# Other slots for the attention visits in the first looped row of an attention-and-MLP kernel

## The chip, the cores and the metric

The kernel runs on one core of a Trainium2 chip. The metric is the device time of one execution in microseconds (us).

## What is computed

The reference has two parts. A linear attention with a decaying state runs over 4 batches, 8 heads, 768 positions and 48 channels, all in float32:

```python
for t in range(S):
    cur = u * k[t] (outer) v[t]
    y[t] = r[t] @ (state + cur)
    state = w[t][:, None] * state + k[t] (outer) v[t]
```

Its output, as 3072 rows of 384, goes through a gated MLP: `(sigmoid(x @ w_gate) * (x @ w_val)) @ w_out`, with 1536 hidden columns.

## The kernel before

**Chunks and rows.** The attention is cut into 24 chunks of 128 positions of one batch. Chunk q belongs to batch q % 4 and to row q // 4, so a row of the MLP is four chunks, 512 tokens. Row n of the MLP can only run when the four chunks of row n are done. A prologue, whose order a planner makes from costs and due times (`Plan`, lines 154 to 199, `add` calls of lines 606 to 681), does chunks 0 to 7, prepares chunk 8, brings in chunk 9's data and computes row 0 of the MLP. The change doesn't touch it.

**The loop.** Rows 1 to 5 run in a written-out loop (lines 761 to 786). A row has 12 steps, one for each 128 hidden columns, and a step has four slots. At each slot, work of the attention that was noted for it is issued first; then comes the step's own work: after slot 0 the gate product (`gate`, PE into `pg`, lines 525 and 528) and its sigmoid (ACT, L538); after slot 1 the value product (PE into `pu`), then `hidden` (DVE, L545), `hidden_hi` (ACT, L549) and `hidden_lo` (DVE, L553); after slot 2 the down product of the step before (PE into `po`, L568); after slot 3 nothing. Slots are counted from the start of the first looped row (row 1), 48 to a row. All engines work their queues in the order of issue.

**The attention's work on chunk q+1 and on chunk q.** `prepare(q + 1, early, turn, late, more)` (line 718) issues, at slot `early`, two products on POOL (`bonus1`, `bonus2`, L319 and L322, which read `tok`), `prep_k` on DVE (a scan L339, a reciprocal L343, a product L345, which read and write `pin`) and `fade` (DVE, L351); at slot `turn` the PE transposes `turn_k` (L370 into `pk`) and their copy `take_k` on ACT (L374 into `kT`); at slots `late` and `more` `prep_r` (DVE, L356 and L361), `guard` (ACT, L365), `bonus3` (DVE, L326) and `bonus4` (POOL, L332). A **visit** of chunk q (line 746) is `both(q)`: 160 small PE products (L418, L431 for chunk q; L389, L402 for chunk q+1), then `take_y` (ACT, L476), `mask`, `middle` and `keep` of chunk q+1 (DVE, L458, L469, L473) and, on SP's queue, the loads of `pin` (L301) and `tok` (L306) for chunk q+2. Three slots later come `turn_x` (PE, L481), `take_x` (ACT, L504) and `rest_x` (DVE, L514). `pin` and `tok` have two buffers each, so the load of chunk q+2 waits until the visit of chunk q has read them. `kT` and `eg` have one buffer, and so has the PSUM bank that `pk`, `py` and `px` take in turn.

**The first looped row.** Chunk 8 has no visit before it, so its transposes stand at slot 1 and its scores and sums (`section1`, L389 and L402) at slot 3 (lines 739 to 742). Four weight blocks are still to be split there: `w_hi` (ACT, L284) and `w_lo` (DVE, L287) at slots 1 and 2, 5 and 6, 9 and 10, 13 and 14 (lines 756 to 758). In rows 2 to 5 the visits stand at slots 7, 19, 31 and 43 of the row, and each chunk is prepared at 7, 5, 3 and 3 slots before the visit that needs it. Row 1 has a table of its own:

```python
visit = {q: (q - start) // B * row + (7 + 12 * (q % B) if q >= start + B else FIRST[q - start]) for q in range(start, NG)}
...
prepare(q + 1, *EARLY[q - start] if q < start + B else (time - 7, time - 5, time - 3, time - 3))
```

Of the kernel before, what the change touches and what calls it, by code (L numbers as in the profile page):

```python
# [41 lines left out]
LATE = dict(b3=-1.05, wl=-28.0, xl=26.5)  # L42
ROOM = dict(pin=2, tok=2, bon=2, eg=1, ready=2, mid=1, kT=1, at=2, pair=1, bank=1, x=2, temp=1, pg=1, pu=1, unit=2)
R0 = 1
FIRST = [11, 21, 32, 43]
EARLY = [(4, 6, 8, 8), (12, 16, 17, 17), (23, 27, 28, 28), (34, 38, 39, 39)]
HC = C // 2
HALVES = [slice(0, HC), slice(HC, C)]
HW = 3 * DM // 2
# [155 lines left out]
def tile_kernel(ctx: ExitStack, tc: tile.TileContext, dec: bass.AP, tok: bass.AP, wts: bass.AP, u: bass.AP, out: bass.AP):  # L205
# [509 lines left out]
    def at(time, f, *a):  # L715
        todo.setdefault(time, []).append((f, a))

    def prepare(q, early, turn, late, more):
        at(early, bonus1, q)
        at(early, bonus2, q)  # L720
        at(early, prep_k, q)
        at(early, fade, q)
        at(turn, turn_k, q)
        at(turn, take_k, q)
        at(late, prep_r, q)
        at(late, guard, q)
        at(more, bonus3, q)
        at(more, bonus4, q)
# [8 lines left out]
    start = (R0 + 1) * B  # L737
    visit = {q: (q - start) // B * row + (7 + 12 * (q % B) if q >= start + B else FIRST[q - start]) for q in range(start, NG)}
    at(1, turn_k, start)
# [3 lines left out]
    for q, time in visit.items():  # L743
        if q + 1 < NG:
            prepare(q + 1, *EARLY[q - start] if q < start + B else (time - 7, time - 5, time - 3, time - 3))
        at(time, both, q)
# [78 lines left out]
```

## Time and profile before

| | us |
|---|---|
| median of 3 runs | 583.19 (582.59 to 584.51) |
| profiled execution, its own time | 585.22 |
| span of its instructions | 582.9 |
| PE busy | 547.9 (94%) |
| DVE busy | 324.0 (56%) |
| ACT busy | 204.7 (35%) |
| POOL busy | 100.7 (17%) |
| mean granted TensorE clock | 0.991 |

PE is TensorE's matmul, PEld its weight load, DVE VectorE, ACT ScalarE, POOL GpSimd, SP SyncE, whose queue issues the loads. L568 is line 568 of the kernel. A tile's name stands without its buffer number. An arrow is read "written from"; "<-" behind an idle time names what ended it. All times within the trace are counted from the first instruction.

### The profile page before, as it was taken

How to read it: one execution, taken by the hardware profiler on the slowest of the kernel's cores; microseconds unless marked ns; L12 is line 12 of the kernel's file. 1: busy time of each engine (PE TensorE's matmuls, PEld its weight loads, DVE VectorE, ACT ScalarE, POOL GpSimd, SP SyncE). 2: the span in 40 equal slices, each digit the busy share in tenths (PEclk: the TensorE clock that was granted, in tenths of full speed). 3: DMA queues.
4: the chain of work that ended last, by engine and by line, in shares of the span. 5: the costliest groups of instructions: out<-in, count | busy, mean ns of one | idle time of the engine just before them, and what ended most of it. 6: DMA issues, size and time to landing. Idle time of an engine off the chain costs nothing.

```text
span 582.9 us, 13165 instructions
## 1 busy us (share of the span) xinstructions
PE 547.9 (94%) x5864; PEld 449.3 (77%) x5864; DVE 324.0 (56%) x451; ACT 204.7 (35%) x376; POOL 100.7 (17%) x89
## 2 busy tenths in 40 slices
PE   3698899999889999999999999999999999999995
PEld 2577687887767888877888888888888888888884
DVE  4998999996754654644535545645545521222221
ACT  2557765744432323422223333223323322321221
POOL 4350533104010210210121221211220200000000
PEclk9999999999898999999999999999999999999998
DMA  8748827324020232231130330230330200100001
GB/s 253 256 170 284 251 93 305 76 77 147 12 90 15 76 89 60 84 90 40 51 90 12 110 113 13 77 90 15 112 107 19 72 3 1 55 1 1 0 1 60
DMA packets 11044, 50.57 MB, mean 87 GB/s; under 512 B 1265, under 2 KB 1266, under 8 KB 9442
## 3 DMA queue, kind: packets, MB, share of 16 engines
q1 hardware_dynamic: 8818, 45.70, 25.0%
q10 hardware_dynamic: 2160, 3.93, 1.7%
q8 instruction: 48, 0.79, 0.6%
q14 instruction: 18, 0.15, 0.1%
HBM read 44.91 MB, written 4.72 MB: 85 GB/s over the span
## 4 chain that ended last, share of the span: by engine, by line
PE 86%; DVE 6%; DMA 3%; issue 2%; ACT 1%; POOL 1%; SPq 0%; DVEq 0%; ACTq 0%
PE po L568 24%; PE pg L525 16%; PE pu L525 15%; PE pg L528 8%; PE pu L528 8%; PE py L431 3%; PE py L418 3%; DMA pin<-dec 3%; PE pg L522 2%; PE pk L370 2%; PE pa L389 2%; PE pa L402 1%; PE px L481 1%; DVE raw L275 1%; PE po L564 1%
## 5 line engine op out<-in xcount | busy, mean ns | idle before, releaser
L545 DVE TENSOR_TENSOR sg<-pu,sg 128x512 f32<-128x512 f32 (+1 forms) x76 | 50.3, 661 | 166.8 <-PE pu L528 162.1
L568 PE MATMUL po<-hh,w 128*128 128x512 f32 x408 | 130.3, 401 | 0.0
L525 PE MATMUL pg<-x,w 128*128 128x512 f32 x408 | 107.5, 399 | 0.0
L525 PE MATMUL pu<-x,w 128*128 128x512 f32 x408 | 105.0, 393 | 0.0
L525 PEld LDWEIGHTS pu<-x,w 128*128 128x128 f32 x408 | 76.8, 189 | 16.2
L525 PEld LDWEIGHTS pg<-x,w 128*128 128x128 f32 x408 | 74.9, 188 | 16.2
L568 PEld LDWEIGHTS po<-hh,w 128*128 128x128 f32 x408 | 75.1, 190 | 14.2
L549 ACT CAST hh<-sg 128x512 fp32r<-128x512 f32 x68 | 42.2, 620 | 123.0 <-DVE sg L545 122.9
L538 ACT ACTIVATE sg<-pg 128x512 f32<-128x512 f32 (+1 forms) x76 | 43.5, 572 | 115.2 <-PE pg L528 110.8
L568 PE MATMUL po<-hl,w 128*128 128x512 f32 x204 | 80.2, 393 | 0.1
L553 DVE TENSOR_TENSOR hl<-sg,hh 128x512 fp32r<-128x512 f32 x68 | 50.2, 738 | 42.2 <-ACT hh L549 42.2
L319 POOL TENSOR_TENSOR bon<-tok,ub 128x384 f32<-128x384 f32 x24 | 30.7, 1280 | 237.1 <-DMA tok<-tok 170.7
L528 PE MATMUL pg<-x,w 128*128 128x512 f32 x204 | 58.3, 394 | 0.0
L528 PE MATMUL pu<-x,w 128*128 128x512 f32 x204 | 57.6, 390 | 0.0
L332 POOL TENSOR_TENSOR at<-eye,a 128x512 f32<-128x512 f32 x24 | 31.5, 1314 | 126.2 <-DVE a L326 126.2
L568 PEld LDWEIGHTS po<-hl,w 128*128 128x128 f32 x204 | 38.6, 189 | 9.2 <-DVE hl L553 0.6
L528 PEld LDWEIGHTS pg<-x,w 128*128 128x128 f32 x204 | 38.7, 190 | 8.4
L528 PEld LDWEIGHTS pu<-x,w 128*128 128x128 f32 x204 | 38.3, 188 | 8.0
L339 DVE TENSOR_TENSOR_SCAN eg<-pin,ends 112x516 f32<-112x516 f32 x24 | 34.7, 1446 | 9.5 <-DMA pin<-dec 9.5
L365 ACT ACTIVATE eg<-eg 112x1032 f32<-112x1032 f32 x24 | 25.6, 1067 | 31.1 <-DVE pin L361 29.8
L322 POOL TENSOR_TENSOR bon<-bon,tok 128x384 f32<-128x384 f32 x24 | 35.5, 1480 | 1.9
L476 ACT COPY bon<-py 128x384 f32<-128x384 f32 x24 | 11.5, 478 | 63.7 <-PE py L431 63.7
(78 smaller groups left out, 646.5 us busy)
## 6 DMA issues: line engine op xcount, KB each, us to landing
pin<-dec SPq DMA_DIRECT2D x23, 675.5 KB, 5.9
tok<-tok SPq DMA_DIRECT2D x24, 576.0 KB, 5.8
raw<-wts SPq DMA_DIRECT2D x12, 1152.0 KB, 10.6
y<-o ACTq DMA_DIRECT2D x15, 256.0 KB, 2.0
y<-o SPq DMA_DIRECT2D x3, 256.0 KB, 3.2
pin<-dec SPq DMA_DIRECT2D x1, 448.0 KB, 3.8
pin<-dec SPq DMA_DIRECT2D x1, 227.5 KB, 2.8
line<-u SPq DMA_DIRECT2D x1, 1.5 KB
```

Of the source, the lines that this page charges most:

```text
L319: nc.gpsimd.tensor_tensor(out=bon[q], in0=tk[q][:, 0:DM], in1=ub, op=ALU.mult)
L322: nc.gpsimd.tensor_tensor(out=bon[q], in0=bon[q], in1=tk[q][:, DM:2 * DM], op=ALU.mult)
L332: nc.gpsimd.tensor_tensor(out=att[q], in0=eye.unsqueeze(1).unsqueeze(1).broadcast_to(shape), in1=a0, op=ALU.mult)
L339: nc.vector.tensor_tensor_scan(out=e[:, 516:0:-1], data0=t[:, 516:0:-1], data1=ends[:, 516:0:-1], initial=0.0, op0=ALU.mult, op1=ALU.add,)
L365: nc.scalar.activation(both, both, AF.Square, accum_out=acc_d[:, q:q + 1])
L525: nc.tensor.matmul(t, lhsT=w[f][:, cols], rhs=x[n][:, a, k, spot], start=k == 0 and j == 0, stop=False)
L528: nc.tensor.matmul(t, lhsT=whi[f][:, cols], rhs=x[n][:, 1, k, i0 * C:i1 * C], start=False, stop=k == NKT - 1)
L538: nc.scalar.activation(sg, hid["g", n, f, i0], AF.Sigmoid)
L545: nc.vector.tensor_tensor(out=sg, in0=hid["u", n, f, i0], in1=sg, op=ALU.mult)
L549: nc.scalar.copy(hh, hid["s", n, f, i0])
L553: nc.vector.tensor_tensor(out=hl, in0=hid["s", n, f, i0], in1=hid["hi", n, f, i0].bitcast(F32), op=ALU.subtract)
L568: nc.tensor.matmul(to, lhsT=w[f][:, cols], rhs=h, start=first and i == 0, stop=last and i == 2, skip_group_check=True)
```

## The change

Two tables of slots are replaced. Before, the visits of chunks 8 to 11 stood at slots 11, 21, 32 and 43; now they stand at 7, 19, 31 and 43, the last slot of steps 2, 5, 8 and 11, counted from 1. Chunk 9 was prepared at slots 4, 6, 8 and 8 (the second and third step), now at 0, 2, 4 and 4 (the first and second). The loads of chunks 10, 11 and 12 go with the visits of chunks 8, 9 and 10; that of chunk 13 stays.

```diff
-FIRST = [11, 21, 32, 43]
-EARLY = [(4, 6, 8, 8), (12, 16, 17, 17), (23, 27, 28, 28), (34, 38, 39, 39)]
+FIRST = [7, 19, 31, 43]
+EARLY = [(0, 2, 4, 4), (11, 14, 16, 16), (23, 26, 28, 28), (35, 38, 40, 40)]
```

## Rows read from the trace of the kernel before

**Rows 1.** Stretches: length, busy PE, PEld, DVE, ACT, POOL, granted clock, DMA share, GB/s.

```profile
152.99:156.40 3.41, 3.41 (x11) 2.83 (x12) 2.73 (x5) 1.05 (x2) 0.00 (x0) 0.50 0.02 5
...
180.30:250.00 69.70, 69.70 (x811) 57.31 (x812) 37.01 (x53) 21.62 (x42) 11.18 (x9) 1.00 0.23 68
```

**Rows 2.** The page: granted TensorE clock in 40 slices of 14.6 us, in tenths.

```profile
PEclk9999999999898999999999999999999999999998
```

**Rows 3.** Chain of waits, first steps of row 1: start, length, what.

```profile
145.53 0.62 PE pa L389 x32
...
151.04 1.90 issue
152.95 0.95 PE pk L370 x4
153.89 3.30 PE po L568 x9
...
161.29 2.04 PE po L568 x9
163.33 0.18 PE py L418
```

**Rows 4.** Timeline of DVE in the first two steps.

```profile
145.64 0.69 DVE L545 TENSOR_TENSOR sg<-pu,sg 128x512 f32<-128x512 f32 x1 [4.38 <-ACT sg L538]
147.68 0.69 DVE L553 TENSOR_TENSOR hl<-sg,hh 128x512 fp32r<-128x512 f32 x1 [1.35 <-ACT hh L549]
148.28 1.35 DVE L287 TENSOR_TENSOR w<-raw,w 128x1152 fp32r<-128x1152 f32 x1
...
150.83 1.22 DVE L339 TENSOR_TENSOR_SCAN eg<-pin,ends 112x516 f32<-112x516 f32 x1
...
152.18 0.66 DVE L345 TENSOR_TENSOR pin<-pin,eg 112x512 f32<-112x512 f32 x1
152.76 0.35 DVE L351 TENSOR_TENSOR ready<-state,eg 112x192 f32<-112x192 f32 x1
```

**Rows 5.** Chain of waits, from the load of chunk 10 to undisturbed steps.

```profile
164.93 5.00 DMA pin<-dec
...
176.15 1.88 PE pg L525 x6
178.03 1.28 PE pg L528 x3
179.31 1.89 PE pu L525 x6
...
192.66 0.33 PE px L481 x3
192.98 1.40 PE pg L525 x6
194.38 0.69 PE pg L528 x3
195.07 1.37 PE pu L525 x6
...
199.18 0.38 PE pk L370 x4
```

**Rows 6.** Timeline of PE at the second wait.

```profile
175.55 0.60 PE L370 MATMUL pk<-ident,pin 112*128 112x112 f32 x4 [3.12 <-DVE x L514]
```

**Rows 7.** Timeline of PE in the prologue: a wait at full clock.

```profile
70.00 0.29 PE L431 MATMUL py<-tok,at 64*32 64x48 f32 x9 [1.27 <-issue]
```

**Rows 8.** Line L301, the load of chunk 9 issued at 136.86: time to landing.

```profile
DMA to landing us min/median/max: 7.0/7.0/7.0
```

**Rows 9.** Line L306, seven loads of tok, the first issued at 165.77.

```profile
DMA to landing us min/median/max: 4.7/5.7/6.6
```

**Rows 10.** Timeline, all engines: a product on POOL beside one on DVE.

```profile
171.71 1.13 POOL L319 TENSOR_TENSOR bon<-tok,ub 128x384 f32<-128x384 f32 x1 [11.88 <-DMA tok<-tok]
...
171.89 1.16 DVE L351 TENSOR_TENSOR ready<-state,eg 112x192 f32<-112x192 f32 x1
```

**Rows 11.** Line L301, two loads issued at 92.7 and 93.2.

```profile
DMA to landing us min/median/max: 13.1/13.9/14.7
```

## The prediction

> **What bounds the kernel now.** I read the stretches first. From 180.3 to 250 us PE is busy in 69.70 of 69.70 us at full clock, while DVE and ACT work a half and a third of the time [rows 1]; three visits of the first looped row, with their loads, lie in there and cost PE nothing but their own products. So PE is the bound, and only what makes PE wait or slows its clock counts. The page's clock row shows two dents, near 150 and near 180 us [rows 2], both in the first looped row, which begins at about 141 us. The chain of waits then gives what stands ahead of each dent.
>
> **First wait.** At 151.04 PE wants the transposes of chunk 9 (slot 6) and idles 1.90 us [rows 3]; the trace names only "issue", but DVE's timeline shows the cause: the product that the transposes read, last part of `prep_k`, runs from 152.18 to 152.84, and PE starts 0.11 us later [rows 4]. DVE is late because `prep_k` stands behind the split of a weight block and the masking of chunk 8. Then 3.41 us run at half clock, 1.2 GHz [rows 1]: the transposes take 0.95 instead of 0.38 [rows 3, 5], the down product 3.30 instead of 2.04 [rows 3]. In all 1.90 + 0.57 + 1.26 = 3.73 us.
>
> **Second wait.** The visit of chunk 8 starts at 163.33 [rows 3]. It frees the buffer for chunk 10, whose load is issued at 164.93, 1.60 us into the visit, and lands 5.00 us later [rows 5]. The old table asks for that chunk one slot after the visit, so DVE stands until 169.93 with the step's own `hidden` and `rest_x` behind it; PE idles 3.12 us before chunk 10's transposes, which wait for the PSUM bank that `rest_x` gives back [rows 6]. Then half clock again: the transposes 0.60 for 0.38, the gate product 1.88 + 1.28 for 1.40 + 0.69, the six value products 1.89 for 1.37 [rows 5, 6]. In all 3.12 + 0.22 + 1.07 + 0.52 = 4.93 us. Both waits together: 8.66 us. I find no other idle PE in this row.
>
> **What the change removes and adds.** No product, copy or load is added; all of it is moved. I number the steps from 0.
>
> Chunk 9's `prep_k` moves from behind step 1's masking to the head of DVE's queue in step 0, where DVE idles for 4.38 us before `hidden` at 145.64 [rows 4]. It can't start before its load is there: issued at 136.86, landed after 7.0 us [rows 8], so at 143.86. From the scan's start to the product's end it takes 152.84 - 150.83 = 2.01 us [rows 4], so it ends at 145.9 and PE could start the transposes (now slot 2) at 146.0. PE comes for them at 145.53 [rows 3]: **a wait of 0.5 us**. Bounds: nothing, were the load 0.5 us sooner; 1.2 us, if the scan and the product are slowed by POOL, which takes chunk 9's products as before when `tok` lands (below). I take 0.6, nearest the undisturbed rows, and add 0.2 for the slower start after a wait (0.60 for 0.38, above): 0.8. Does the clock fall? After 1.27 us of waiting in the prologue it stayed full [rows 2, 7]; after 1.90 it fell. With 0.6 I say it stays.
>
> Behind the waiting scan stand `fade` (0.35) and step 0's `hidden`, which then starts near 146.3 instead of 145.64; `hidden_lo` starts at 147.68 anyway, since ACT has a weight cast ahead of `hidden_hi`, so that delay ends there.
>
> Chunk 9's copy on ACT now stands ahead of chunk 8's sums on PE, and `kT` has one buffer. I expect the copy to wait for those sums, not the other way; on ACT only work of step 1 stands behind it. Price nothing, since PE waits for none of it before the visit.
>
> `prep_r` of chunk 9 comes where `prep_k` stood, at 150.9, and needs about 2 us like it: 152.9. PE reaches the visit of chunk 8, now slot 7, at 151.04 plus about 1.1 (the transposes and their wait come first now) plus 2.04 for the down product, 154.2: cover 1.3 us. `guard`, the sigmoid and `hidden_lo` of step 1 shift by up to 3 us behind it, but PE needs them only after the visit and step 2's gate and value products, over 6 us later.
>
> Chunk 10: let v be the end of step 2's value product, which is 2.4 (visit) plus 2.09 and 2.05 after the visit's start. The load, issued 1.60 into the visit, lands 5.0 to 7.0 later [rows 5, 8], at v + 0.1 to v + 2.1. DVE asks for it after `hidden`, a wait for `hidden_hi`, `hidden_lo` (0.7 each), `rest_x` (0.5) and the last but one weight block (1.3) [rows 4], at v + 3.9: **the 5 us load is hidden**, cover 1.8 us. `prep_k` is done at v + 5.9. PE comes for the transposes at v + 0.33 + 2.04 + 2.09 + 2.05 = v + 6.5 [rows 3, 5]: cover 0.5 us. But POOL takes chunk 10's products when `tok` lands, 4.7 to 6.6 us after the visit's end [rows 9], v + 0.6 to v + 2.5, beside exactly this DVE work, and a small DVE product beside POOL took 1.16 instead of 0.35 [rows 4, 10]. One such loss of 0.8 gives a wait of 0.3, two give 1.1, none gives 0. I take 0.3 and 0.2 for the start: 0.5.
>
> The Trainium skill, GPSIMD Engine Reference, section Specifications, says that GpSimd shares its SBUF interfaces with VectorE and collides with instructions that have two SBUF inputs. The trace agrees [rows 4, 10]. By that rule every DVE product next to POOL is slowed, which would put this wait at its upper end, 1.1 us.
>
> The visits of chunks 9 to 11 and their loads get 12 slots between them where 10 or 11 were, and the distances of the later rows, which show no wait [rows 1]; I cost them at nothing. On SP's queue nothing but these loads stands behind a visit's wait. **Sum: 8.66 - 0.8 - 0.5 = 7.4 us saved**, bounds 8.66 - 2.7 = 6.0 and 8.66 if no wait is left. The profiled execution took 585.22 us (span 582.9 and 2.3 around it), 2.0 above the median; the waits are taken to be the same in both: 577.8 in a profiled execution, **575.8 us** for the median. What is saved reaches the end whole, since PE has no slack behind this row that could take it back.
>
> **Rivals.**
>
> (a) The clock falls at chunk 10's transposes: POOL's overlap costs DVE two or three slowed instructions, PE waits 1.3 or more instead of 0.3, and the half-clock stretch follows, 1.8 us by both cases above (0.57 + 1.26, 0.22 + 1.07 + 0.52). For it: cover of only 0.5. Against: the wait for `hidden_hi` takes in part of the overlap. Then 575.8 + 1.0 + 1.8 = 578.6. Chance 0.12.
>
> (b) The same at chunk 9's transposes in step 0: 1.3 us of lateness more (load or scan), so a wait of 1.9, and 1.8 of half clock: 578.9. For it: this load was slower than that of chunk 10. Against: everything before it is unchanged. Chance 0.09.
>
> (c) Chunk 8's sums wait for chunk 9's copy in the one `kT` buffer. ACT can't begin that copy before `hidden_hi` is done at about 147.7 [rows 4], so PE loses at least 1.1 us more, with the half clock 2.9: 576.9 to 578.7. Against: the sums read the older tile. Chance 0.06.
>
> (d) Slower: chunk 9's load is late. With `prep_k` at the head of DVE's queue, whatever it is late by stops step 0 itself, where before 7 us of slack lay behind its landing. Two loads took 13.1 and 14.7 us beside weight transfers [rows 11]; with 14.7 it lands at 151.6, PE waits till 153.7, 8.2 us, and with the half clock 1.8 and the second wait 0.5 the sum is 10.5 against 8.66: 585.0. It decides once the load takes over 12.9 us. Only three output stores of row 0 and chunk 9's `tok` run beside it. Chance 0.03.
>
> (e) The change doesn't do what it says: the new places carry waits as long as the old, both with a fall of the clock, 583. Chance 0.03.
>
> **How the numbers follow.** Forecast 0.67, of itself 574.5 to 577.0; (a) to (e) take the rest. A difference of 0.3%, 1.7 us, is about what a measurement of this kernel can tell from no change. Forecast, (a), (b) and (c) are all faster by more: 0.94; same 0.03 from (e); slower 0.03 from (d). The range goes from 574.5, both waits gone, to 578.9, which takes in (a) to (c).
>
> **What would show it.** Right: PE idle near 145.6 by about 0.5 us, no idle before the transposes of chunk 9 at step 1 (they are gone from there), the scan of chunk 10 starting with no DMA named before it, a clock row without the two dents, the first looped row some 7.4 us shorter and the later rows as before. Wrong: a half-clock stretch within the first four steps, DVE still ended by the load of `pin`, or a saving in the row that rows 2 to 5 give back.

## The result and the profile after

The changed kernel took 578.0 us (median of 8 runs, 576.9 to 579.9) against 583.1 (8 runs, 582.0 to 587.6): a ratio of 0.9895, 95% interval 0.9867 to 0.9923. In a second set of runs it took 578.1 against 582.9, ratio 0.9928 (0.9902 to 0.9955). So it is some 4 to 6 us faster by the two ratios, 2.6 to 7.8 by their intervals; 7.4 had been forecast. One execution of the kernel before, of 590.6 us, counts as slow, over 1.5% above the fastest, and is left out of what follows.

The profiled execution took 577.0 us, span 575.3, against 585.2 and 582.9: 8.2 less, more than the medians differ. Where the 7.6 us of the span came from is read off the starts of the rows, each the start of the row's first gate product in the trace (us):

| execution | row 1 starts | row 1 | row 2 | row 3 | row 4 | row 5 to the end |
|---|---|---|---|---|---|---|
| before | 140.9 | 95.60 | 89.72 | 87.17 | 86.55 | 83.01 |
| changed | 140.6 | 88.33 | 89.69 | 87.17 | 86.56 | 82.94 |

All but 0.4 us of it, 7.27 us, lies in the first looped row. The page's clock row has lost its two dents, which stand in [rows 2]:

```profile
PEclk9999999999999999999999999999999999999998
```

The stretches of that row, with the columns of [rows 1], show PE idle for 0.5 us in the first and 0.6 in the second, always at full clock:

```profile
140.60:160.00 19.40, 18.91 (x295) 15.40 (x294) 12.76 (x20) 11.05 (x18) 3.08 (x3) 1.00 0.35 104
160.00:181.00 21.00, 20.38 (x243) 16.61 (x242) 14.04 (x19) 7.13 (x13) 4.25 (x3) 1.00 0.15 45
181.00:228.90 47.90, 47.90 (x518) 39.49 (x518) 24.81 (x37) 13.90 (x28) 8.69 (x7) 1.00 0.25 71
```

The two waits, in PE's timeline, before the transposes of chunk 9 and of chunk 10; the second answers to [rows 6], the first to the 1.90 us of [rows 3]:

```profile
145.73 0.51 PE L370 MATMUL pk<-ident,pin 112*128 112x112 f32 x3 [0.49 <-ACT kT L374]
...
167.60 0.58 PE L370 MATMUL pk<-ident,pin 112*128 112x112 f32 x4 [0.62 <-PE pu L528]
```

What ended the first is not what had been forecast. DVE's timeline shows chunk 9's scan starting at 143.00, as its load landed, and the product that the transposes read ending at 145.12:

```profile
143.00 1.33 DVE L339 TENSOR_TENSOR_SCAN eg<-pin,ends 112x516 f32<-112x516 f32 x1 [2.05 <-DMA pin<-dec]
...
144.46 0.66 DVE L345 TENSOR_TENSOR pin<-pin,eg 112x512 f32<-112x512 f32 x1
```

PE starts 0.6 us after that, when ACT has copied chunk 8's transposes out of the one PSUM bank. ACT's timeline has that copy (145.16 to 145.68) and chunk 9's copy, which waits for chunk 8's sums (L402), not the sums for it:

```profile
145.16 0.52 ACT L374 COPY kT<-pk 128x448 f32<-128x448 f32 x1
...
147.54 0.53 ACT L374 COPY kT<-pk 128x448 f32<-128x448 f32 x1 [0.17 <-PE pa L402]
```

The second wait ends 0.10 us after `prep_k` of chunk 10 on DVE. The weight split there took 1.71 us instead of the 1.35 of [rows 4], the scan 2.04 instead of 1.22; POOL's two products ran from 162.33 to 165.61. The scan has no idle time before it: the load, issued at 155.38, had landed at 160.8. DVE's timeline:

```profile
163.03 1.71 DVE L287 TENSOR_TENSOR w<-raw,w 128x1152 fp32r<-128x1152 f32 x1
164.66 2.04 DVE L339 TENSOR_TENSOR_SCAN eg<-pin,ends 112x516 f32<-112x516 f32 x1
...
166.83 0.67 DVE L345 TENSOR_TENSOR pin<-pin,eg 112x512 f32<-112x512 f32 x1
```

And POOL's, over the same stretch:

```profile
162.33 1.19 POOL L319 TENSOR_TENSOR bon<-tok,ub 128x384 f32<-128x384 f32 x1 [8.23 <-DMA tok<-tok]
163.60 2.01 POOL L322 TENSOR_TENSOR bon<-bon,tok 128x384 f32<-128x384 f32 x1
```

So the trace bears out the sum (7.27 against 7.4), and yet the medians lie only some 5 us apart. The experiments ask what the other executions do.

### The profile page after: what moved, and what is told of

It reads as the page before. It is cut to its first block, busy times and chain, and to the rows that moved or that the text cites. A ratio compares the mean times of both kernels' runs of the same rounds, so it can differ in the third digit from the quotient of the medians.

```text
span 575.3 us, 13167 instructions
## 1 busy us (share of the span) xinstructions
PE 545.3 (95%) x5864; PEld 448.0 (78%) x5864; DVE 323.5 (56%) x451; ACT 204.3 (36%) x376; POOL 103.9 (18%) x89
## 4 chain that ended last, share of the span: by engine, by line
PE 87%; DVE 5%; DMA 3%; issue 2%; ACT 1%; POOL 1%; SPq 0%; ACTq 0%; DVEq 0%
PE po L568 23%; PE pg L525 16%; PE pu L525 16%; PE pu L528 8%; PE pg L528 8%; PE py L431 3%; PE py L418 3%; DMA pin<-dec 3%; PE pk L370 2%; PE pa L389 2%; PE pg L522 1%; PE pa L402 1%; PE px L481 1%; PE pu L522 1%; PE po L564 1%
## 5 line engine op out<-in xcount | busy, mean ns | idle before, releaser
L553 DVE TENSOR_TENSOR hl<-sg,hh 128x512 fp32r<-128x512 f32 x68 | 49.2, 724 | 42.5 <-ACT hh L549 42.5
L319 POOL TENSOR_TENSOR bon<-tok,ub 128x384 f32<-128x384 f32 x24 | 30.4, 1266 | 230.3 <-DMA tok<-tok 200.4
L322 POOL TENSOR_TENSOR bon<-bon,tok 128x384 f32<-128x384 f32 x24 | 39.1, 1628 | 1.9
L339 DVE TENSOR_TENSOR_SCAN eg<-pin,ends 112x516 f32<-112x516 f32 x24 | 35.2, 1469 | 6.9 <-POOL line L248 3.9
```

The costliest lines, as they stand in the source:

```text
L319: nc.gpsimd.tensor_tensor(out=bon[q], in0=tk[q][:, 0:DM], in1=ub, op=ALU.mult)
L322: nc.gpsimd.tensor_tensor(out=bon[q], in0=bon[q], in1=tk[q][:, DM:2 * DM], op=ALU.mult)
L339: nc.vector.tensor_tensor_scan(out=e[:, 516:0:-1], data0=t[:, 516:0:-1], data1=ends[:, 516:0:-1], initial=0.0, op0=ALU.mult, op1=ALU.add,)
L553: nc.vector.tensor_tensor(out=hl, in0=hid["s", n, f, i0], in1=hid["hi", n, f, i0].bitcast(F32), op=ALU.subtract)
```

## The experiments

Each run lists span and mean granted clock of every execution. Span times (1 - clock) is the time that half clock cost in it; the clock is given to 0.001, so one execution is known to 0.3 us, and part of it comes from the kernel's end, where the clock also falls: 1.2 to 2.4 us in the ten traces.

**The kernels again.**

> The changed kernel once more, with five rounds beside the kernel before. Theory A (both waits of the profiled execution, each with its half-clock stretch, stand in every execution of the kernel before): 7.4 us under the kernel before. Theory B (the waits stand in every execution, but the clock falls behind them only in some, and the profiled execution of before had both falls): 3.9 us under it without a fall, 5.7 with one, 7.4 with both, so a median near 5. In the trace of this run under either: waits of about 0.5 and 0.6 us before the transposes of chunks 9 and 10, no half-clock stretch in the first looped row.

Measured: 578.1 against 582.9, 2.6 to 5.7 us less by the interval, so the 7.4 of theory A lies outside. In the trace waits of 0.59 and 0.84 us, no half clock in row 1, row 1 88.65 us.

> The kernel before, unchanged, for a second trace of it and the granted clock of more executions. Theory A (a wait of 1.9 or 3.1 us always drops the clock): two half-clock stretches of 3.4 us in the first looped row, as in the first trace, row of 95.6 us, mean granted clock near 0.990 in every execution. Theory B (the wait is there each time, the fall only sometimes): waits of about 1.9 and 3 us at the same transposes in any case, a row of 92.0 us without a fall, 93.8 with one, 95.6 with two, and mean clocks between 0.990 and 0.998.

Measured: 585.4 against 583.2 of its companions (the same kernel), no difference that can be told (ratio 1.0011, 0.9977 to 1.0045). The new trace of before, PE's timeline at the two waits:

```profile
154.90 0.29 PE L370 MATMUL pk<-ident,pin 112*128 112x112 f32 x1 [1.93 <-issue]
...
177.64 0.64 PE L370 MATMUL pk<-ident,pin 112*128 112x112 f32 x2 [3.23 <-DVE x L514]
```

The stretches at half clock around them, with the columns of [rows 1]:

```profile
156.00:159.40 3.40, 3.40 (x9) 2.64 (x8) 3.05 (x3) 0.75 (x2) 0.00 (x0) 0.50 0.00 0
176.50:183.30 6.80, 5.66 (x16) 4.60 (x17) 4.65 (x6) 1.59 (x5) 1.05 (x1) 0.50 0.01 2
```

The same two waits to about 0.1 us, but with the second go 6.8 us at half clock instead of 3.4, and row 1 took 96.94 us. A third fall stands in the prologue of this trace. There PE waits 1.29 us, as it did 1.27 us in the first trace, where the clock stayed full [rows 2, 7]:

```profile
70.04 0.25 PE L431 MATMUL py<-tok,at 64*32 64x48 f32 x5 [1.29 <-issue]
```

The stretch that follows:

```profile
70.66:74.07 3.41, 3.41 (x9) 2.73 (x9) 3.38 (x4) 2.01 (x3) 0.00 (x0) 0.50 0.77 279
```

Over 60 executions of before the mean clock ran from 0.985 to 0.999; the one at 0.999 lost 0.6 us in all, so it can have had no fall in row 1. Over 17 of the changed kernel it ran from 0.993 to 0.998. The cost of half clock, falls in the prologue included, was 4.1 us in the mean before and 2.2 after; the 4.1 is the mean of three sets of runs with 3.7, 3.7 and 5.6, the last being this run's. Theory A falls, B stands, with falls longer than it had allowed for.

**One wait at a time.**

```diff
 kernel before, e3:
-EARLY = [(4, 6, 8, 8), (12, 16, 17, 17), ...
+EARLY = [(0, 2, 4, 4), (12, 16, 17, 17), ...
 kernel before, e4:
-EARLY = [(4, 6, 8, 8), (12, 16, 17, 17), ...
+EARLY = [(4, 6, 8, 8), (15, 18, 18, 18), ...
```

> The kernel before with chunk 9 prepared at slots 0, 2, 4 and 4, and all visits where they were. Takes away the first wait alone. Theory A: 3.73 less 0.7 for the small wait that replaces it, 3.0 us under the kernel before; the second wait of about 3 us stands before the transposes of chunk 10, with its half clock. Theory B: 1.3 us without, 3.0 with a fall of the clock at the old place.

Measured: no gain, 583.1 against 582.9, ratio 1.0002 (0.9974 to 1.0031). PE's timeline has two small waits where the 1.9 us was, the second a new one, and the old second wait:

```profile
146.37 0.32 PE L370 MATMUL pk<-ident,pin 112*128 112x112 f32 x1 [0.36 <-ACT kT L374]
...
154.87 0.50 PE L525 MATMUL pg<-x,w 128*128 128x512 f32 x1 [0.47 <-ACT sg L538]
...
173.41 0.60 PE L370 MATMUL pk<-ident,pin 112*128 112x112 f32 x4 [3.02 <-DVE x L514]
```

The new one comes from `guard`, which holds up step 1's sigmoid on ACT; in the changed kernel the visit of chunk 8 stands there and covers it. After the 3.02 us the clock stayed full, as the stretch behind the wait shows:

```profile
173.40:176.80 3.40, 3.39 (x17) 2.87 (x18) 3.37 (x4) 1.12 (x3) 0.00 (x0) 1.00 0.02 5
```

But that is this execution: 6 of the 12 had a mean clock of 0.992 or less, as had 21 of 60 of before. Row 1 took 91.39 us, against 92.2 for before without its falls (95.60 less 3.41, half of the two stretches of 3.41 us at half clock). The 92.0 of the expectations took off 0.22 more, the transposes' 0.60 for 0.38; but they take 0.60 at full clock here too, at 173.41. So the first wait alone is worth 0.8 us in the trace, not the 3.0 of A, and nothing that the runs can tell.

> The kernel before with chunk 10 prepared at slots 15, 18, 18 and 18 in place of 12, 16, 17 and 17, its visit and load where they were, so that the load has landed when DVE asks for it. Takes away the second wait alone. Theory A: 4.9 us under the kernel before; the first wait of about 1.9 us stays, with its half clock. Theory B: 3.2 us without, 4.9 with a fall of the clock at the old place. If the load were not the cause of the second wait, nothing changes.

Measured: 580.2 against 582.9, ratio 0.9946 (0.9920 to 0.9973), 1.6 to 4.7 us less. Row 1 took 90.02 us, 2.2 less than the 92.2, and the first wait stands, in PE's timeline:

```profile
154.02 0.29 PE L370 MATMUL pk<-ident,pin 112*128 112x112 f32 x1 [1.91 <-issue]
```

The stretch behind it is at full clock:

```profile
154.00:157.40 3.40, 3.38 (x17) 2.89 (x18) 2.71 (x5) 1.05 (x2) 0.00 (x0) 1.00 0.02 5
```

None of its 12 executions had a clock of 0.992 or less; half clock cost 2.3 us in the mean. So the second wait caused most of the falls, and asking for the load later, with nothing else moved, takes it away. Of the 3.12 us, 0.62 came back at the same transposes.

**The two small waits.**

```diff
 changed kernel, e2 and e7:
-EARLY = [(0, 2, 4, 4), (11, 14, 16, 16), ...
+EARLY = [(0, 3, 4, 4), (10, 14, 16, 16), ...
```

> The changed kernel with the transposes of chunk 9 one slot later (3, behind the scores and sums of chunk 8) and the preparation of chunk 10 one slot earlier (10, ahead of the weight block's split on DVE). If the two small waits cost what their rows show, 0.49 and 0.62 us with about 0.2 each for the start after it, this takes 1.1 to 1.5 us off the changed kernel, and PE has no wait over 0.1 us between the start of the first looped row and its end. Rival: chunk 10's load, landed 2.3 us before its scan in the changed kernel, is asked for 1.7 us sooner and still lands in time; if it does not, a wait of up to 1 us comes back at the same transposes.

> The kernel with the transposes of chunk 9 at slot 3 and the preparation of chunk 10 from slot 10, once more on another chip. First looped row 86.8 us, against 88.3 to 88.7 of the changed kernel; 576 us, 7 us under the kernel before.

Measured: 575.3 (ratio to before 0.9865, 0.9825 to 0.9906) and 576.7 (0.9889, 0.9841 to 0.9937), 6 runs each, better than the kernel before; against the changed kernel the mean of the twelve is 576.1, that of its seventeen 578.3. PE has no wait over 0.1 us left in row 1, which took 86.82 and 87.02 us, 1.3 to 1.8 less than the changed kernel's; both small waits were worth what their rows show and a little more. The stretch of the whole row in the second trace:

```profile
139.50:226.60 87.10, 87.06 (x1053) 71.72 (x1052) 51.53 (x77) 31.88 (x58) 15.55 (x13) 1.00 0.24 73
```

**POOL beside DVE.** In the changed kernel POOL's first product of chunk 10 gets a dependency on the last product of that chunk's `prep_k`, which for that is issued ahead of it.

```diff
+            tc.add_manual_dep(first.ins, product[q].ins.name, sync, ...)
 ...
+        if q == 10:
+            at(early, prep_k, q)
         at(early, bonus1, q)
         at(early, bonus2, q)
-        at(early, prep_k, q)
+        if q != 10:
+            at(early, prep_k, q)
```

> The changed kernel with POOL's two products for chunk 10 held back until DVE has done the last product of that chunk's prep_k, so that they no longer run beside the weight split and the scan on DVE. If POOL beside DVE is the cause of the wait of 0.6 to 0.8 us before chunk 10's transposes, the split takes 1.35 us instead of 1.7, the scan 1.23 instead of 2.04, the wait is gone and the first looped row is 0.8 us shorter than the changed kernel's 88.3 to 88.7 us. If the cause is the amount of DVE work alone, the wait stays at 0.6 us.

Measured: 577.4 us, ratio to before 0.9886 (0.9843 to 0.9929); row 1 87.71 us, 0.6 to 0.9 less than the changed kernel's. The second wait is gone, the first is 0.68. DVE's timeline (in this kernel L319 is L321, and the lines from L322 on are 5 higher):

```profile
163.50 1.35 DVE L287 TENSOR_TENSOR w<-raw,w 128x1152 fp32r<-128x1152 f32 x1
164.76 1.23 DVE L344 TENSOR_TENSOR_SCAN eg<-pin,ends 112x516 f32<-112x516 f32 x1
```

POOL's timeline, with the product of DVE that now releases it:

```profile
167.02 1.01 POOL L321 TENSOR_TENSOR bon<-tok,ub 128x384 f32<-128x384 f32 x1 [12.47 <-DVE pin L350]
168.10 1.01 POOL L327 TENSOR_TENSOR bon<-bon,tok 128x384 f32<-128x384 f32 x1
```

So POOL's overlap is the cause of the second wait: with it away, split and scan are back to 1.35 and 1.23, and POOL's own second product takes 1.01 instead of 2.01.

**A longer wait.**

```diff
 changed kernel, e8:
-EARLY = [(0, 2, 4, 4), ...
+EARLY = [(0, 1, 4, 4), ...
```

> The changed kernel with the transposes of chunk 9 one slot earlier (1, straight behind those of chunk 8, which hold the one PSUM bank until ACT has copied them). That copy, at 145.7 us in the changed kernel, lets PE go on: a wait of about 2.6 us before the second transposes instead of 0.5, in step 0. Theory A: the clock falls behind it each time, first looped row 2.1 plus 1.8, 3.9 us longer than the changed kernel's. Theory B: 2.1 us longer, and 1.8 more only in some executions, so that the mean granted clock of the executions is spread, more than the changed kernel's and less than the kernel before's.

Measured: 582.5 us, the whole gain lost (ratio to before 0.9990, 0.9959 to 1.0021). PE waits 2.77 us:

```profile
143.48 0.45 PE L370 MATMUL pk<-ident,pin 112*128 112x112 f32 x1 [2.77 <-ACT kT L374]
```

Half clock begins within that wait and lasts 6.8 us; it cost 4.0 us in the mean of 12 executions, 0.990 to 0.996, as spread as B says. But row 1 is 94.63 us, about 6 longer than the changed kernel's, more than either theory gave: the half clock costs 3.1 in this trace (half of the 6.15 us in which PE was busy in it), and a consequence neither had is in ACT's timeline. Chunk 9's copy, moved up with its transposes, stands 6.7 us waiting for chunk 8's sums, with the step's `hidden_hi` behind it; DVE is late in turn, and PE waits 0.99 us more, at the visit of chunk 8, for `prep_r`.

```profile
150.16 0.53 ACT L374 COPY kT<-pk 128x448 f32<-128x448 f32 x1 [6.73 <-PE pa L402]
...
151.71 0.62 ACT L549 CAST hh<-sg 128x512 fp32r<-128x512 f32 x1
```

The stretch at half clock:

```profile
142.81:149.63 6.82, 6.15 (x67) 4.83 (x70) 0.76 (x2) 0.61 (x2) 0.00 (x0) 0.50 0.10 38
```

## Why the prediction was right, and what it missed

**Right:** the direction, the place and the waits, and the range, though this in part by luck: 574.5 to 578.9 held 578.0, but the forecast's own part of it ended at 577.0, and the rest had been added for rivals (a) to (c), none of which came as told. The load of chunk 10 is hidden: it landed at v + 0.3 (v, the end of step 2's value product, is 160.5) and DVE asked at v + 4.2; forecast v + 0.1 to 2.1 and v + 3.9. Two small waits were forecast, 0.6 and 0.3; 0.49 and 0.62 came, 0.59 and 0.84 in the second trace. Later rows differed by 0.07 us or less between the two profiled executions. The clock didn't fall at the small waits in either trace; one of the 17 executions, at 0.993, lost 4.0 us, more than the end takes in any trace, so in some it may have.

**What failed: "the waits are taken to be the same in both"**, profiled execution and median. The waits are the same, but of the 8.66 us counted as saved 3.4 were half clock (3.64 by the prediction's terms), and that is not in every execution: after the same 1.9 us the clock fell in both traces of before and not in e4's, after the same 3.0 to 3.2 us it fell in both traces of before, for 3.4 and for 6.8 us, and not in e3's. The mean execution of before lost 4.1 us to half clock, of which the kernel without waits in the row (e2 and e7) still loses 1.7; so the falls in row 1 and the prologue together cost about 2.4 us in the mean, and 0.5 of it stays in the changed kernel. The sum with the measured terms: without falls row 1 goes from 92.2 to 88.3 or 88.65, 3.7 us, and half clock from 4.1 to 2.2, 1.9 in the mean: 5.6, against 5.1 between the means of all executions (583.4 of 60 before, 578.3 of 17 after). That the profiled execution stood 2.0 us over the median was seen and not used; with two falls in it, it was one of the slower ones.

**Right size by luck, wrong cause:** the first small wait was put down to the load of chunk 9. The load was 0.7 us sooner (6.3 us) than in the trace of before, and what PE waited for was the PSUM bank, which ACT empties at 145.68; the prediction named the bank for chunk 10 only. e2 puts the transposes behind chunk 8's sums and the wait goes, but that edit gives both causes time, so the row of ACT is what tells them apart.

**Misread rows.** "After 1.27 us of waiting in the prologue it stayed full [rows 2, 7]; after 1.90 it fell" was taken as a line between waits that keep the clock and waits that lose it. It is none: in the second trace of before the clock fell after 1.29 us in the same place, and in e4's it held after 1.91. The transposes' 0.60 for 0.38 at the second wait was counted as half clock there, and further on as the slower start after a wait. It is the latter: they ran from 175.55, and the clock fell at 176.88. And "the later rows, which show no wait [rows 1]" goes beyond that stretch, which ends at 250: PE waits 1.02 and 1.08 us in row 2 of the same trace. The changed kernel has these waits too (1.17 and 0.94).

**Mis-sized:** the second wait, 0.3 forecast. POOL slowed two DVE instructions, not one, by 0.36 and 0.8; the upper bound of 1.1 had this case, with 0.8 for each. The rule cited from the Trainium skill, GPSIMD Engine Reference, section Specifications, named the right instructions: those with two SBUF inputs collide with GpSimd, and both slowed ones have two; e6 agrees, with 1.35 and 1.23 us once POOL is away. But "every DVE product next to POOL is slowed", as the prediction read it, goes too far: the scan of e7 shown in the last section ran beside POOL in its undisturbed 1.22 us.

**The rivals.** (a) came half way: the wait was longer, the clock held in both traces. (b) and (d) didn't come: the load was on time. (c) is refuted by ACT's row: the copy waits for the sums. (e) is refuted by the row's length.

## What to carry to other kernels

A stall's price in one trace has a fixed part, the idle time, and a part that comes and goes, the clock that falls behind it. Take the second from the mean granted clock of several executions, not from the one that was profiled, and see first whether that one stands above or below the median. When work is pulled forward, list for each of its instructions every tile it waits for, the one-buffer bank that an earlier consumer still holds as well as its data; and look at what POOL runs beside DVE there.

## What the runs showed of the hardware that was not expected

The same wait of PE, 1.9 us, was followed in one execution by 1.2 GHz and in another by 2.4 GHz throughout, and a stretch at half clock was 3.4 us or 6.8 us long. In the second trace of before the clock had fallen at 176.5, while PE stood idle (174.4 to 177.6); in the first it fell at 176.9, 1.3 us after PE had gone on.

When a product of POOL and a DVE instruction with two SBUF inputs overlapped, the one that started second took longer. In the changed kernel the split (163.03) came behind POOL's first product and took 0.36 us longer; POOL's second product (163.60) came behind the split and took 2.01 instead of 1.01; the scan (164.66) came behind that and took 2.04 instead of 1.22. In e7 the scan came first, and only POOL paid, 1.47 instead of 1.01:

```profile
161.49 1.22 DVE L339 TENSOR_TENSOR_SCAN eg<-pin,ends 112x516 f32<-112x516 f32 x1
162.05 1.47 POOL L319 TENSOR_TENSOR bon<-tok,ub 128x384 f32<-128x384 f32 x1 [8.81 <-DMA tok<-tok]
```

Between 138 and 235 us of the ten traces there are 135 overlaps of over 0.2 us between POOL's L319 or L322 and DVE's L287, L339, L345, L351 or L553; all go this way.

Rows 3 and 4 took the same time to 0.01 us in all ten traces. What varied from trace to trace, besides the falls, was the prologue (row 1 starts at 138.1 to 142.6 us), row 5 with the end (82.9 to 84.0 us) and row 2 (89.6 to 91.0 us), where PE stands 0.9 to 1.7 us, by the trace for "issue", within the visits of chunks 12 and 13. The change doesn't touch these, and the cause was not tried.
